# Partial sums of every second row tile of the fifth product kept in spare room of that product's w2 tiles

## The chip, the cores and the metric

The kernel runs on one core of a Trainium2 chip. The metric is the device time of one execution, in microseconds (us): the median of a few runs, and beside it one profiled execution whose trace shows every instruction. TensorE is called PE here, VectorE DVE, ScalarE ACT, GpSimd POOL, and SyncE, which mostly issues transfers, SP.

## What is computed

```python
xn = _layernorm(x)                                    # x: 1 x 2048 x 1024
s  = irfft2(rfft2(xn) * (w_r + 1j * w_i))             # a filter in the Fourier domain
g  = silu(silu(xn @ w1) @ w2)                         # w1: 1024 x 3584, w2: 3584 x 1024
return x + s * g
```

The change lies in the second matrix product of g, `h @ w2`, where h is `silu(xn @ w1)`.

## The kernel before

**The second product as seven.** `h @ w2` is not done in four blocks of 512 columns and half the rows, but by Strassen's scheme as seven smaller products, m = 0 to 6, of sums and differences of blocks. Each works on eight row tiles j = 0 to 7 of 128 rows and 512 columns. For each tile PE runs 42 matmuls into one PSUM tile `pb` (L539 to L541: 14 slices, three matmuls each, because operands are split into a high and a low f16 half): 21 with chunk k = 0 of the weights, 21 with chunk k = 1. Between the two chunks and after the second, other work may be put in.

**Weights.** `w2_gen` loads each slice of w2 into a tile `jr` (L412), and splits it: ACT writes the high half (L251, called from `split`), DVE the low half (L254). The halves go into `w2t[m, 0]` and `w2t[m, 1]`, seven slices each, in a ring of four buffers with the tag "big". The ring's buffers were made for `xnT` (2 x 8 x 512 f16, 16 KB in each partition), and a w2 tile of seven slices takes 14 KB of one. Two tiles to a product and four buffers to the ring: a tile of product 6 (the seventh) goes into the buffer that a tile of product 4 (the fifth) had. So the first write into `w2_6_0`, the split of slice 84 (`jr84`), must come after the last use of `w2_4_0`. The weights of product 6 are prepared while product 5 runs, and the first of those splits already during the last row tile of product 4.

**Partial sums.** In the fifth product, m = 4, each row tile adds its result to two earlier partial sums (`READS[4]` is (1, 0)). `load_parts` has SP load both from DRAM into tiles of 128x512 f32 (`pl`, L532): k = 1 (`pl4_j_1`, from `pd1_j`) and k = 0 (`pl4_j_0`, from `pd0_j`). DVE adds the PSUM tile to both (L596, L597). The k = 1 sum goes on through silu (L632), a product with the filter's result and an addition of x, and out (L626). The k = 0 sum goes back to `pd0_j` (L577, called from `keep`), to be used once more in product 6. Both tiles come from a ring of six, tag "pt". A row tile takes two of them, so a buffer comes back three row tiles later, and the load into it waits for the store out of it.

**The Fourier work beside it.** During products 0 to 6 a background queue feeds in the inverse transform. One pass over it (`i_gen`) has four first matmul groups `iu` (24 matmuls each, L1204 or L1212) into a ring of two PSUM tiles. Each group is evacuated by ACT (`uc`, L1218) and then by DVE (`ub`, L1220 and L1221). After some DVE arithmetic (`uu`), ACT writes the high half of `us` (L1283) and DVE the low half (L1284). Four second groups `id` (L1294) read all four `us` tiles. The third `iu` group can start only when DVE has emptied the first one's PSUM tile, and the fourth when the second one's is empty.

**Order and queues.** The order on each engine is fixed when the program is built: a rule feeds background work by estimated PE and DVE clocks. Stores are put off by a number of steps (`store`, `tick`): that of a k = 0 sum by three. Each engine runs its list in order, and a waiting instruction holds up what stands behind it. SP's transfers go on one queue, in the order of its list, and ACT issues the loads of h (`ht`, L515) in between its own work. Every transfer of SP or ACT reports to one of eight counters, DMAHW0 to DMAHW7; a wait in the lists below names the counter.

Of the kernel before, what the change touches and what calls it, by code (L numbers as in the profile page):

```python
# [9 lines left out]
F16 = mybir.dt.float16  # L10
F32 = mybir.dt.float32
# [116 lines left out]
def spectral_ffn(ctx, tc, x, w_r, w_i, w1, w2, ca, kc, ci, tw, pm, out):  # L128
    nc = tc.nc
# [12 lines left out]
    fp = ctx.enter_context(tc.tile_pool(name="fp", bufs=1))  # L142
    hstack = ExitStack()
    H = {"p": hstack.enter_context(tc.tile_pool(name="hid", bufs=1))}
    pf = ctx.enter_context(tc.tile_pool(name="pf", bufs=4, space=PSUM))
    pt = ctx.enter_context(tc.tile_pool(name="pt", bufs=2, space=PSUM))
# [5 lines left out]
    pd = {(k, j): dp.tile([128, 512], F32, name=f"pd{k}_{j}") for k in range(3) for j in range(8)}  # L152
# [38 lines left out]
    def store(tag, n, fn):  # L191

        d = [n, None]

        def run():
            held[tag].remove(d)
            fn()

        d[1] = run
        held.setdefault(tag, []).append(d)  # L200
        deferred.append(d)

    def tile_of(pool, shape, dtype, name, tag, bufs):
        while len(held.get(tag, ())) >= bufs - 1:
            d = held[tag][0]
            deferred.remove(d)
            d[1]()
        return pool.tile(shape, dtype, name=name, tag=tag, bufs=bufs)
# [35 lines left out]
    xnT, w1t, h32, w2t = {}, {}, {}, {}  # L244
# [5 lines left out]
    def high(hi, raw, scale):  # L250
        nc.scalar.activation(hi, raw, AF.Copy, scale=scale)  # L251

    def low(lo, raw, scale, hi):
        nc.vector.scalar_tensor_tensor(lo, raw, scale, hi, op0=OP.mult, op1=OP.subtract)  # L254
# [144 lines left out]
    def w2_block(m, q, b):  # L399
        r, h = W2_BLOCKS[m][b]  # L400
        return w2[(2 * q + r) * 128:(2 * q + r + 1) * 128, h * 512:(h + 1) * 512]

    def w2_gen():

        todo = [(m, q) for m in range(7) for q in range(NP)]
        raw = {}

        def load(n):
            if n < len(todo):
                m, q = todo[n]  # L410
                raw[n] = J["p"].tile([128, 512], F32, name=f"jr{n}", tag="jr", bufs=6)
                nc.sync.dma_start(raw[n], ws[m][q] if m in ws else w2_block(m, q, 0))  # L412

        def join(n):
            if n < len(todo) and todo[n][0] in SUMMED:
                nc.gpsimd.dma_start(raw[n], w2_block(*todo[n], 1), accum_op=OP.add)

        def split(n):
            m, q = todo[n]
            if q % 7 == 0:  # L420
                w2t[m, q // 7] = fp.tile([128, 7, 2, 512], F16, name=f"w2_{m}_{q // 7}", tag="big", bufs=4)
            high(w2t[m, q // 7][:, q % 7, 0], raw[n], sc2[:, q:q + 1])

        def rest(n):
            m, q = todo[n]
            w = w2t[m, q // 7][:, q % 7]
            low(w[:, 1], raw.pop(n), sc2[:, q:q + 1], w[:, 0])
            ready2[0] = n

        for n in range(4):  # L430
            load(n)
        yield 0
        yield 0
        for n, (m, q) in enumerate(todo):
            while q % 7 == 0 and (done2[0] < m - 1 or chunks[0] <= (3 if m else q // 7) and m < 2):
                if n and ready2[0] < n - 1:
                    rest(n - 1)
                yield 0
            load(n + 4)
            join(n + 2)  # L440
            split(n)
            if n and ready2[0] < n - 1:
                rest(n - 1)
            yield 0.1
        rest(n)
# [78 lines left out]
    def home(m, j):  # L524
        return ("kept", 8) if m == 6 and j >= 4 else ("pt", 6)

    def load_parts(m, j):
        for k in READS[m]:
            if (k, j) in part:
                continue  # L530
            t_ = tile_of(H["p"], [128, 512], F32, f"pl{m}_{j}_{k}", *home(m, j))
            nc.sync.dma_start(t_, pd[k, j])  # L532
            part[k, j] = t_

# [24 lines left out]
    def ahead_rows(m, j):  # L559
        g, p = j // 4, j % 4  # L560
        for c, h in FINALS[m]:
            tags = (("kept", 8), ("kept", 8)) if m == 6 else (("fs", 3), ("fx", 2))
            if m == 6 and j >= 4:
                tags = (("kept", 8), ("fs", 3) if h else ("fx", 2) if j < 7 else ("pt", 6))
            if (2 * g + c, p) in stile and (2 * g + c, p, h) not in rows:
                rows[2 * g + c, p, h] = rows_for(2 * g + c, p, h, H["p"], tags)

    def acc(m, j, ps, cols=slice(0, 512)):
        tt = nc.vector.tensor_tensor
        g, p = j // 4, j % 4  # L570
        ahead_rows(m, j)

        def fresh(name):
            return tile_of(H["p"], [128, 512], F32, f"{name}_{j}", "pt", 6)

        def keep(k, t_):
            store("pt", 3, lambda: nc.sync.dma_start(pd[k, j], t_))  # L577

        def evac():
            if m == 0:  # L580
                kept[j] = H["p"].tile([128, 512], F32, name=f"kept{j}", tag="kept", bufs=8)
                nc.scalar.activation(kept[j], ps, AF.Copy)
            elif m == 1:
                t_ = fresh("c11")
                tt(t_, kept[j], ps, op=OP.subtract)
                keep(0, t_)
            elif m == 2:
                tt(kept[j], kept[j], ps, op=OP.add)
            elif m == 3:
                t_ = fresh("c21")  # L590
                nc.scalar.activation(t_, ps, AF.Copy)
                tt(kept[j], kept[j], ps, op=OP.subtract)
                keep(1, t_)
            elif m == 4:
                t_, u = part.pop((1, j)), part.pop((0, j))
                tt(t_, t_, ps, op=OP.add)  # L596
                tt(u, u, ps, op=OP.add)  # L597
                keep(0, u)
                return final(2 * g + 1, p, 0, t_)
            elif m == 5:  # L600
                t_ = fresh("c12")
                nc.scalar.activation(t_, ps, AF.Copy)
                tt(kept[j], kept[j], ps, op=OP.add)
                keep(2, t_)
                return final(2 * g + 1, p, 1, kept.pop(j))
            else:
                t_, u = part[2, j][:, cols], part[0, j][:, cols]
                tt(t_, t_, ps, op=OP.subtract)  # L608
                tt(u, u, ps, op=OP.add)
                tag = home(m, j)[0]  # L610
                a_, b_ = final(2 * g, p, 1, t_, cols, tag), final(2 * g, p, 0, u, cols, tag)

                def both():
                    x_, y_ = a_(), b_()
                    return (lambda: (x_ and x_(), y_ and y_(), None)[2]) if x_ or y_ else None

                return both

        return evac
# [8 lines left out]
    def final(c, p, h, o, cols=slice(0, 512), tag=None):  # L628
        tag = tag or ("kept" if h and c % 2 else "pt")

        def act():
            nc.scalar.activation(o, o, AF.Silu, scale=c2)  # L632
            if (c, p) not in stile:
                store(tag, 1, lambda: nc.sync.dma_start(gd[c, p, h], o))
                fins[c, p, h] = True
                return None
            t_ = rows.get((c, p, h)) or rows_for(c, p, h, H["p"], (("fs", 3), ("fx", 2)))
            return lambda: finish_out(tag, c, p, h, o, *(v[:, cols] for v in t_), cols)

        return act  # L640
# [778 lines left out]
    with tc.manual_schedule():  # L1419
# [134 lines left out]
        for n, (m, j) in enumerate(seq):  # L1554
# [14 lines left out]
            for k in range(2):  # L1569
                while ready2[0] < m * NP + 7 * k + 6:  # L1570
                    slot(wq)
                mm2(m, j, ps, k)
                if k == 0:
                    settle()
                    load_parts(m, j)
                    ahead_rows(m, j)
                    if (m, j) == (6, 6):
                        load_parts(m, 7)
                        ahead_rows(m, 7)
                    tick()  # L1580
                    work()
# [43 lines left out]
```

## Time and profile before

| | |
|---|---|
| median of 3 runs | 1237.54 us (1236.69 to 1238.83) |
| the profiled execution | 1235.84 us, of which 1234.1 us span |
| DVE busy | 999.0 us, 81% of the span |
| ACT busy | 467.6 us, 38% |
| product 4 (the fifth) on PE | from about 984 to 1063 us of the span |
| moved by DMA | 293.67 MB, 238 GB/s on average |
| transfers `pd<-pl` in this stretch (8), issue to landing | 3.2 to 7.7 us, median 6.5 |

Times in the rows of a trace count from the start of the span. A row of a timeline gives the start, the length, the engine, the line and the operation, and in brackets the idle time of the engine before it with what ended that. A matmul's length is modelled, and matmuls overlap; for PE the distance from start to start counts.

### The profile page before, as it was taken

What the parts mean: (1) busy time and instruction counts of PE and PEld (TensorE: products, weight loads), DVE (VectorE), ACT (ScalarE), POOL (GpSimd) and SP (SyncE); (2) the same over time, 40 slices, a digit from 0 to 9 for tenths busy, and PEclk for the clock granted to TensorE, in tenths of its full rate; (3) what the DMA queues carried; (4) which work ended last, traced back from release to release, by engine and by line L of the source; (5) the groups of instructions that cost most, each with busy time, mean ns of one, the idle gap of its engine ahead of it and who ended that gap; (6) DMA issues with size and microseconds to landing.
All of it is one profiled execution on the core that took longest, in us unless ns stands there. A gap on an engine that the chain in (4) does not pass through costs nothing.

```text
span 1234.1 us, 19097 instructions
## 1 busy us (share of the span) xinstructions
PE 1220.7 (99%) x7033; PEld 625.2 (51%) x7033; DVE 999.0 (81%) x1970; ACT 467.6 (38%) x614; POOL 117.3 (10%) x245
## 2 busy tenths in 40 slices
PE   8999999999999999999999999999999999999998
PEld 5545445444544454445545555554455555555545
DVE  7687988899798898896969899985186678798886
ACT  4865344333554565444433222122032222243212
POOL 2330000001000000010001121114111111000000
PEclk9999999999999999999999999999999999999999
DMA  7487476655758898759898999997989999998576
GB/s 253 134 172 187 135 224 201 185 152 161 223 172 237 276 283 242 217 177 279 207 283 224 283 259 198 276 256 246 293 207 278 286 289 331 315 332 325 200 261 260
DMA packets 271102, 293.67 MB, mean 238 GB/s; under 512 B 40096, under 2 KB 198816, under 8 KB 270624
## 3 DMA queue, kind: packets, MB, share of 16 engines
q1 hardware_dynamic: 250992, 233.66, 65.7%
q10 hardware_dynamic: 15984, 51.45, 12.0%
q0 software_dynamic: 4032, 7.34, 3.5%
q8 instruction: 55, 0.90, 0.3%
q14 instruction: 39, 0.32, 0.1%
HBM read 185.95 MB, written 102.25 MB: 234 GB/s over the span
## 4 chain that ended last, share of the span: by engine, by line
PE 75%; DVE 11%; DMA 9%; issue 2%; ACT 1%; SPq 0%; POOL 0%; DVEq 0%; ACTq 0%; POOLq 0%
PE pa L456 45%; PE pb L539 8%; PE pb L541 8%; PE pb L540 8%; DVE Z L1055 2%; DMA wq<-in_A_w_i_dram 2%; DMA sd<-s 2%; PE id L1294 2%; DMA zd<-zq 1%; DMA ht<-hd_sum_d 1%; DVE T L1020 1%; DVE w L254 1%; PE iu L1204 1%; ACT xp L709 1%; PE iu L1212 1%
## 5 line engine op out<-in xcount | busy, mean ns | idle before, releaser
L456 PE MATMUL pa<-xnT,w 128*128 128x512 f16 x2688 | 585.2, 379 | 1.1 <-ACT w L251 0.7
L456 PEld LDWEIGHTS <-w 128*128 128x128 f16 x2688 | 262.2, 98 | 311.6 <-DVE w L254 1.3
L539 PE MATMUL pb<-w,ht 128*128 128x512 f16 (+2 forms) x812 | 300.4, 372 | 0.0
L540 PE MATMUL pb<-w,ht 128*128 128x512 f16 (+2 forms) x812 | 300.4, 372 | 0.0
L541 PE MATMUL pb<-w,ht 128*128 128x512 f16 (+2 forms) x812 | 300.3, 372 | 0.0
L541 PEld LDWEIGHTS <-ht 128*128 128x128 f16 x812 | 79.4, 98 | 91.0
L539 PEld LDWEIGHTS <-ht 128*128 128x128 f16 x812 | 79.5, 98 | 86.7
L540 PEld LDWEIGHTS <-ht 128*128 128x128 f16 x812 | 79.4, 98 | 86.7
L465 ACT ACTIVATE h<-pa,s 128x512 f32<-128x512 f32 x112 | 75.5, 678 | 122.9 <-PE pa L456 111.0
L251 ACT ACTIVATE w<-jr,sc 128x512 f16<-128x512 f32 x98 | 68.1, 713 | 77.8 <-PE pb L541 22.1
L254 DVE SCALAR_TENSOR_TENSOR w<-jr,sc,w 128x512 f16<-128x512 f32 x98 | 71.1, 744 | 2.1 <-ACT w L251 2.1
L254 DVE SCALAR_TENSOR_TENSOR hoone<-h,hs,hoone 128x2048 f16<-128x2048 f32 x28 | 65.6, 2344 | 7.9 <-ACT hoone L251 7.9
L251 ACT ACTIVATE hoone<-h,hs 128x2048 f16<-128x2048 f32 x28 | 56.0, 1998 | 36.5 <-DVE h L499 24.3
L251 ACT ACTIVATE hosum<-hr,hs 128x1536 f16<-128x1536 f32 x28 | 44.1, 1574 | 64.1 <-DVE hr L495 26.8
L981 ACT ACTIVATE zq<-Z,zs 128x1024 f16<-128x1024 f32 x16 | 18.4, 1149 | 103.9 <-DVE Z L1055 57.0
L494 DVE TENSOR_TENSOR hr<-h 128x1024 f32<-128x1024 f32 x28 | 34.2, 1221 | 24.4 <-ACT h L465 24.3
L254 DVE SCALAR_TENSOR_TENSOR hosum<-hr,hs,hosum 128x1536 f16<-128x1536 f32 x28 | 50.7, 1812 | 3.1 <-ACT hosum L251 3.1
L251 ACT ACTIVATE w<-w1r,rs 128x1024 f16<-128x1024 f32 x28 | 31.9, 1144 | 47.0 <-DVE w L254 31.8
L274 DVE TENSOR_REDUCE m<-w1r 128x1 f32<-128x1024 f32 x28 | 33.8, 1210 | 16.1 <-DMA w1r<-in_B_w_dram 16.1
L632 ACT ACTIVATE pl<-pl,c 128x512 f32<-128x512 f32 (+2 forms) x28 | 17.6, 657 | 70.1 <-DVE pl L608 41.6
L954 PE MATMUL fx<-vq,kq 128*128 128x256 f16 x192 | 43.2, 273 | 0.0
L955 PE MATMUL fx<-vq,kq 128*128 128x128 f16 x192 | 42.0, 219 | 0.0
(219 smaller groups left out, 1524.8 us busy)
## 6 DMA issues: line engine op xcount, KB each, us to landing
w1r<-in_B_w_dram SPq DMA_DIRECT2D x28, 512.0 KB, 6.2
hd_sum<-hosum SPq DMA_DIRECT2D x56, 256.0 KB, 2.9
hd_one<-hoone SPq DMA_DIRECT2D x56, 256.0 KB, 3.7
hd_dif<-hoone SPq DMA_DIRECT2D x56, 256.0 KB, 3.2
w2m<-in_B_w_dram SPq DMA_DIRECT2D x28, 512.0 KB, 5.2
ht<-hd_dif ACTq DMA_DIRECT2D x32, 448.0 KB, 6.3
jr<-in_B_w_dram SPq DMA_DIRECT2D x56, 256.0 KB, 6.8
ht<-hd_sum ACTq DMA_DIRECT2D x32, 448.0 KB, 6.4
```

Of the source, the lines that this page charges most:

```text
L251: nc.scalar.activation(hi, raw, AF.Copy, scale=scale)
L254: nc.vector.scalar_tensor_tensor(lo, raw, scale, hi, op0=OP.mult, op1=OP.subtract)
L274: nc.vector.tensor_reduce(m1[:, i:i + 1], raw[i], axis=AX.XY, op=OP.max, apply_absolute_value=True)
L456: nc.tensor.matmul(ps, w[:, wh, d], xt[:, xh, d], start=(n == 0), stop=(n == 23))
L465: nc.scalar.activation(hq[:, 2 * (c % 2) + f % 2], ps, AF.Silu, scale=s1[:, f:f + 1])
L494: tt(sums[:, 0:2], hq[:, 0::2], hq[:, 1::2], op=OP.subtract)
L539: nc.tensor.matmul(ps, hh[:, 0], w[:, 0], start=first, stop=False)
L540: nc.tensor.matmul(ps, hh[:, 0], w[:, 1], start=False, stop=False)
L541: nc.tensor.matmul(ps, hh[:, 1], w[:, 0], start=False, stop=last)
L954: nc.tensor.matmul(o, k[:, c, kh, 1], v[:, c, vh], start=(n == 0), stop=False)
L955: nc.tensor.matmul(ps[:, c, 0], k[:, c, kh, 2], v[:, c, vh, 128:256], start=False, stop=False)
L1055: eng.tensor_tensor(Z[:, ns, pos], x0[:, :, ls], x1[:, :, ls], op=o_)
```

## The change

The w2 tiles get room for an eighth slice, which no weight uses: 2 x 512 f16 in each partition, as many bytes as 512 f32. In product 4, for odd j, the k = 0 partial sum is loaded into that room instead of a tile of the "pt" ring: j = 1 and 5 into `w2_4_0`, j = 3 and 7 into `w2_4_1`. Its store back to DRAM is counted under the tag "big". The ring's buffers stay 16 KB.

```diff
         def split(n):
             m, q = todo[n]
             if q % 7 == 0:
-                w2t[m, q // 7] = fp.tile([128, 7, 2, 512], F16, name=f"w2_{m}_{q // 7}", tag="big", bufs=4)
+                w2t[m, q // 7] = fp.tile([128, 8, 2, 512], F16, name=f"w2_{m}_{q // 7}", tag="big", bufs=4)
...
         for k in READS[m]:
             if (k, j) in part:
                 continue
-            t_ = tile_of(H["p"], [128, 512], F32, f"pl{m}_{j}_{k}", *home(m, j))
+            if m == 4 and k == 0 and j % 2:
+                t_ = w2t[m, j // 2 % 2][:, 7].rearrange("p h x -> p (h x)").bitcast(F32)
+            else:
+                t_ = tile_of(H["p"], [128, 512], F32, f"pl{m}_{j}_{k}", *home(m, j))
             nc.sync.dma_start(t_, pd[k, j])
             part[k, j] = t_
...
         def keep(k, t_):
-            store("pt", 3, lambda: nc.sync.dma_start(pd[k, j], t_))
+            store("big" if m == 4 and j % 2 else "pt", 3, lambda: nc.sync.dma_start(pd[k, j], t_))
```

The instructions of all five engines stay the same, in the same order; line numbers behind L531 grow by three. What changes is which buffer some transfers use, and so what instructions wait for. Two places show it.

SP's list, from the second load for row tile 6 of product 4 (`pl4_6_0`) to the store of the k = 0 sum of row tile 5 (`pd0_5`). Before:

```order
L532 DMA pl4_6_0_10397<-pd0_6_104 128x512 [waits DMAHW6_49]
L556 DMA fs3_2_0_10399<-sd3_2_136 128x512 [waits DMAHW4_49]
L556 DMA fx3_2_0_10401<-in_A_x_dram 128x512 [waits DMAHW5_49,DVE_49]
L577 DMA pd0_4_102<-pl4_4_0_10137 128x512
L1354 DMA sd3_3_137<-s3_3_10354 128x1024 [waits DMAHW0_49]
L626 DMA out_0_dram<-pl4_4_1_10135 128x512 [waits DMAHW2_49]
L412 DMA jr87_10406<-in_B_w2_dram 128x512 [waits DMAHW3_49,DMASW1_49,Activation_49]
L532 DMA pl4_7_1_10463<-pd1_7_113 128x512 [waits DMAHW6_49,DMAHW4_49]
L532 DMA pl4_7_0_10465<-pd0_7_105 128x512 [waits DMAHW5_49,DMAHW2_49]
L556 DMA fs3_3_0_10467<-sd3_3_137 128x512 [waits DMAHW0_49]
L556 DMA fx3_3_0_10469<-in_A_x_dram 128x512 [waits DMAHW7_49,DVE_49]
L577 DMA pd0_5_103<-pl4_5_0_10304 128x512
```

With the change:

```order
L535 DMA pl4_6_0_10394<-pd0_6_104 128x512 [waits DMAHW3_49]
L559 DMA fs3_2_0_10396<-sd3_2_136 128x512 [waits DMAHW4_49]
L559 DMA fx3_2_0_10398<-in_A_x_dram 128x512 [waits DMAHW5_49,DVE_49]
L580 DMA pd0_4_102<-pl4_4_0_10135 128x512 [waits DMAHW6_49]
L1357 DMA sd3_3_137<-s3_3_10351 128x1024 [waits DMAHW0_49]
L629 DMA out_0_dram<-pl4_4_1_10133 128x512 [waits DMAHW2_49]
L412 DMA jr87_10403<-in_B_w2_dram 128x512 [waits DMAHW3_49,DMASW1_49,Activation_49]
L535 DMA pl4_7_1_10460<-pd1_7_113 128x512 [waits DMAHW4_49]
L535 DMA w2_4_1_9088<-pd0_7_105 128x512 [waits DMAHW5_49]
L559 DMA fs3_3_0_10463<-sd3_3_137 128x512 [waits DMAHW6_49,DMAHW0_49]
L559 DMA fx3_3_0_10465<-in_A_x_dram 128x512 [waits DMAHW7_49,DVE_49]
L580 DMA pd0_5_103<-w2_4_0_8680 128x512
```

Here `fs` and `fx` are rows of the filter's result and of x, `sd` the filter's rows in DRAM. Counted through the program: `pl4_6_0` waited for the store of `out` from row tile 3 (DMAHW6) and now waits for that of `pd0_3`. `pl4_7_1` waited for the store of `pd0_4`, and now waits only for the load `fs3_2`. `fs3_3` reads what the store `sd3_3` (DMAHW0) wrote, before and after. The store of `pd0_5` stands in the same place and waits for nothing of its own.

ACT's list, from the silu of row tile 6, past the evacuation of the second `iu` group, to a load of h (`ht`). Before:

```order
L632 ACTIVATE pl4_6_1_10395<-pl4_6_1_10395,c2_229 128x512 [waits DMAHW3_49]
L251 ACTIVATE w2_6_0_10564<-jr84_10220,sc2_230 128x512 [waits DMAHW6_49]
L1283 ACTIVATE us0_0_10591<-uu0_0_10528 128x1024 [waits DVE_49]
L1218 ACTIVATE uc0_1_10594<-iu0_1_10498 128x512 [waits PE_49,Activation_49]
L1264 ACTIVATE up0_1_10600<-ub0_1_10596 128x8 [waits DVE_49,Activation_49]
L1265 ACTIVATE up0_1_10600<-ub0_1_10596 128x8
L515 DMA ht5_2_0_10611<-hd_one_0_0_94 128x1792 [waits DMAHW4_49]
```

With the change:

```order
L635 ACTIVATE pl4_6_1_10392<-pl4_6_1_10392,c2_229 128x512 [waits DMAHW0_49]
L251 ACTIVATE w2_6_0_10560<-jr84_10218,sc2_230 128x512 [waits DMAHW6_49,DMAHW0_49]
L1286 ACTIVATE us0_0_10587<-uu0_0_10524 128x1024 [waits DVE_49]
L1221 ACTIVATE uc0_1_10590<-iu0_1_10494 128x512 [waits PE_49,Activation_49]
L1267 ACTIVATE up0_1_10596<-ub0_1_10592 128x8 [waits DVE_49,Activation_49]
L1268 ACTIVATE up0_1_10596<-ub0_1_10592 128x8
L515 DMA ht5_2_0_10607<-hd_one_0_0_94 128x1792 [waits DMAHW4_49]
```

The split of slice 84, the first write into `w2_6_0`, waited for its own load (DMAHW6). Now it also waits on DMAHW0 for the count that the store of `pd0_5` completes, since that store reads from the buffer `w2_6_0` is given. In the same way the first split into `w2_6_1`, that of slice 91, now waits for the store of `pd0_7`; `jr91` is loaded two transfers behind that store on SP's queue.

## The prediction

> **What bounds the kernel now.** I read the page's busy shares first, then PE's waits, the stretch of product 4, and the timelines of PE, DVE, ACT and SP around PE's one late wait.
>
> ```profile
> PE 1220.7 (99%) x7033; PEld 625.2 (51%) x7033; DVE 999.0 (81%) x1970; ACT 467.6 (38%) x614; POOL 117.3 (10%) x245
> PE tp L718 <- ACT x L709: 3.0, 3, 2.0
> PE iu L1212 <- DVE ub L1221: 1.7, 1, 1.7
> 984.00:1075.00 91.00, 89.28 (x565) 46.96 (x564) 70.34 (x161) 22.97 (x44) 7.51 (x9) 1.00 0.96 302
> ```
>
> PE is busy for 99% of the span, at full granted clock. Of its waits, the one on `iu` is the only one during the seven products; the others fall near the start, where the change does nothing. So the kernel is a chain of matmuls: an edit can win at most that wait, and loses whatever new gap it makes on PE. In the stretch of product 4 (window, then busy PE, PEld, DVE, ACT, POOL, clock, DMA share, GB/s) the DMA engines are 96% busy. Transfers are slow there.
>
> The old wait, followed back on the chain of waits (start, length, what):
>
> ```profile
> 1049.77 7.96 DMA out_dram<-pl
> 1057.75 3.87 DMA pl<-pd
> 1061.64 0.69 DVE pl L597
> 1062.33 0.60 DVE ub L1220
> 1062.93 0.61 DVE ub L1221
> ```
>
> ```profile
> 1061.48 0.38 PE L541 MATMUL pb<-w,ht 128*128 128x512 f16 x1
> 1063.59 1.55 PE L1212 MATMUL iu<-kk,zt 128*128 128x129 f16 x24 [1.72 <-DVE ub L1221]
> 1074.04 1.54 PE L1212 MATMUL iu<-kk,zt 128*128 128x129 f16 x24
> 1098.07 3.21 PE L1294 MATMUL id<-cis,us 128*128 128x130 f16 x48
> ```
>
> A store lands after 7.96 us and frees a "pt" buffer, the load of `pl4_6_0` starts, the second add of row tile 6 (L597) waits for it, and behind it on DVE stands the evacuation on which the third `iu` group waits. The rows at 1074.04 (fourth `iu` group) and 1098.07 (first two `id` groups) show no wait: they have slack, and the sum turns on how much.
>
> **Term 1, the wait removed.** Odd row tiles take one "pt" tile instead of two, so a buffer comes back later and its store is done.
>
> ```profile
> 1054.94 3.14 SPq L532 DMA_DIRECT2D pl<-pd  x2
> 1048.67 0.51 SPq L577 DMA_DIRECT2D pd<-pl  x1
> DMA to landing us min/median/max: 6.2/6.2/6.2
> DMA to landing us min/median/max: 4.8/4.8/4.8
> 1059.56 0.60 ACT L1218 ACTIVATE uc<-iu 128x512 f32<-128x512 f32 x1 [4.76 <-DMA pl<-pd]
> ```
>
> The first landing is that of the store issued at 1048.67 (`pd0_3`), so 1054.9; the second that of the load issued at 1054.94 (`pl4_6_1`). `pl4_6_0`, issued at 1057.75 before, now waits only for `pd0_3` and starts at 1054.9. At its neighbour's 4.8 us it lands at 1059.7 instead of 1061.6, 1.9 us earlier. L597 can then run at 1059.7, L1220 behind it 0.6 later at 1060.3 (ACT's copy, done at 1060.16, allows it), and PE's group follows at about 1061.6, where it is due at 1061.48 + 0.22. The gap of 1.7 us closes. If the busy queue gives the second load 0.9 us more, 0.8 is won. Bounds: 0.8 to 1.7; I take 1.7. The earlier loads of row tiles 3 to 5 cost or win nothing, since PE waits for none of their users.
>
> **Term 2, the wait added.** The split of slice 84 on ACT now waits for the store of `pd0_5`.
>
> ```profile
> 1063.79 0.71 ACT L632 ACTIVATE pl<-pl,c 128x512 f32<-128x512 f32 x1
> 1064.40 0.71 ACT L251 ACTIVATE w<-jr,sc 128x512 f16<-128x512 f32 x1
> 1066.53 1.06 ACT L1283 ACTIVATE us<-uu 128x1024 f16<-128x1024 f32 x1 [1.42 <-DVE uu L1277]
> 1067.49 0.58 ACT L1218 ACTIVATE uc<-iu 128x512 f32<-128x512 f32 x1
> 1068.75 0.42 SPq L556 DMA_DIRECT2D fs<-sd  x1
> 1069.69 0.43 SPq L577 DMA_DIRECT2D pd<-pl  x1
> DMA to landing us min/median/max: 6.9/6.9/6.9
> ```
>
> Before, the split ran at 1064.40. The store it must now follow was issued at 1069.69 and took 6.9 us: it landed at 1076.6, 12 us after the split. The data were ready long before (row tile 5's adds), but the store is put off three steps and stands on SP behind the loads of row tile 7.
>
> How early can the store be with the change? Ahead of it on SP stands `fs3_3`, which must wait for the store `sd3_3` to land.
>
> ```profile
> 1059.55 0.43 SPq L1354 DMA_DIRECT2D sd<-s  x1
> DMA to landing us min/median/max: 8.2/8.2/8.2
> 1058.13 0.42 SPq L556 DMA_DIRECT2D fs<-sd  x1
> 1049.22 0.51 SPq L1354 DMA_DIRECT2D sd<-s  x1
> DMA to landing us min/median/max: 7.9/7.9/7.9
> ```
>
> `fs3_2` was held until 1058.13 behind `pl4_6_0`; now its own wait, for `sd3_2`, is the last, 1049.22 + 7.9 = 1057.1, so SP is about 1.05 us earlier and `sd3_3` goes out at 1058.5. At 8.2 us it lands at 1066.7. `fs3_3` then starts, and by the distance in the rows above (1068.75 to 1069.69) the store of `pd0_5` 0.9 later, at 1067.6: 2.1 us earlier than before. Its landing, T0:
>
> ```profile
> DMA to landing us min/median/max: 3.2/6.5/7.7
> ```
>
> These are the eight such stores of product 4: T0 lies between 1070.8 and 1075.3. At its own 6.9 it would be 1074.5. But the transfers ahead of it are thinner now, and ACT, being stopped, doesn't issue its `ht` loads beside it; I take 5.7, between the smallest and the own value but nearer to the latter, so T0 = 1073.3. In a sentence by itself: the Trainium skill, "DMA: Bandwidth & Descriptors", section "Anatomy of one DMA — SWDGE (gpsimd) path", puts a DMA of GpSimd's queue at about 2.0 us plus its bytes over 436 GB/s, an estimate of 2.6 us for these 256 KB, by which T0 would be 1070.2 and the total below 3.1 us; the rows of this stretch, on SP's queue, show 6.9 us, and they decide.
>
> What is queued behind the split on ACT: the high half of `us0_0`, the evacuation `uc0_1`, then the `ht` loads for product 5. DVE waits for the first two, PE for DVE.
>
> ```profile
> 1067.62 1.23 DVE L1284 SCALAR_TENSOR_TENSOR us<-uu,us 128x1024 f16<-128x1024 f32 x1 [1.12 <-ACT us L1283]
> 1069.36 0.68 DVE L1221 TENSOR_TENSOR ub<-iu,uc 128x512 f32<-128x512 f32 x1
> 1062.85 0.68 DVE L1221 TENSOR_TENSOR ub<-iu,uc 128x512 f32<-128x512 f32 x1
> 1075.65 0.71 ACT L251 ACTIVATE w<-jr,sc 128x512 f16<-128x512 f32 x1
> 1076.27 1.04 ACT L1283 ACTIVATE us<-uu 128x1024 f16<-128x1024 f32 x1
> 1096.82 1.22 DVE L1284 SCALAR_TENSOR_TENSOR us<-uu,us 128x1024 f16<-128x1024 f32 x1 [1.02 <-ACT us L1283]
> ```
>
> First consequence, the fourth `iu` group. From a split to the next activation 0.62 (1075.65 to 1076.27), from `us` to L1221 of the next group 2.83 (1066.53 to 1069.36), from an L1221 to PE's start 0.74 (1062.85 to 1063.59): PE can start at T0 + 4.2 = 1077.5, against 1074.04 before. That is 3.5 us late (and a visible wait of 5.2, as PE arrives 1.7 early).
>
> Second consequence, the `id` groups. DVE's low half of `us0_0` moves from 1067.62 to T0 + 0.62 + 1.09 = 1075.0, so DVE is 7.4 us late. From there to the low half of `us0_3` at 1096.82 DVE is nearly always busy: its idle gaps are the about 1 us that ACT takes for each `us`, so I let the lag stay whole. `us0_3` is ready at 1098.04 + 7.4 = 1105.4. PE needs it after 18 of the 48 matmuls from 1098.07, that is 1.14 later (18/48 of about 3.05), at 1099.2. The slack is 1.15, and PE ends 7.4 - 1.15 = 6.2 us late: the first wait and a second of 2.7 us together, with term 1 already spent inside them. Bounds from T0 (late = T0 - 1067.1): 3.7 to 8.2.
>
> What is late next (the ending of product 5 on ACT, the landing of `ht` loads in this stretch, the splits on DVE):
>
> ```profile
> L602 ACT ACTIVATE c<-pb x8: 575/597/597, 1080.8 to 1153.0; 128x512 f32<-128x512 f32 x8
> DMA to landing us min/median/max: 3.8/6.6/11.2
> L254 DVE SCALAR_TENSOR_TENSOR w<-jr,sc,w x16: 741/746/752, 1052.0 to 1137.8; 128x512 f16<-128x512 f32 x16
> ```
>
> The late `ht5_2` loads cost nothing: issued at about T0 + 4.3 and landing some 6.6 later, at 1084.2, they are needed when product 5's third row tile starts. From the third `iu` group to the fourth, one group and one row tile of 42 matmuls, it is 10.45; from the fourth the same again leads to 1084.5, and 3.5 late to 1088.0. The wait of slice 91's split costs nothing either: its own load stands behind the same store. The splits of `w2_6` are over by 1138.5, and product 6 starts where ACT empties the last tile of product 5, at 1153: 15 us, which cover the lag.
>
> **Sum.** 1235.84 + 6.2 = 1242.0 for an execution like the profiled one. The median of the runs shown is 1.7 above that execution, so I predict 1243.7.
>
> **The rivals.**
> - *Only the first wait counts* (0.17): DVE makes up its lag before `us0_3`. For it: DVE is 81% busy over the span. Against it: hardly a gap between 1067 and 1097. Time: 1235.84 + 3.5 + 1.7 = 1241.0.
> - *The store is later or the delay spreads* (0.10): `sd3_3` takes the 9 us that such stores reach, `pd0_5` its 7.7, `ht5_2` comes late too. Late = 8.2 + 1, so about 1246.9.
> - *The added wait is covered* (0.13): this is the other side. The store lands before ACT's stop reaches PE; only term 1 is left: 1237.54 - 1.7 = 1235.8, and less if that too comes back as a wait. It decides only if T0 is below 1067.1, which is before the store can be issued by the rows above; it needs SP to be freed some 4 us earlier, by stores that land in 5 us instead of 8. Against it stands the 96% DMA share.
>
> That the change does nothing is no rival: the lists show the wait.
>
> **How the numbers follow.** The forecast, both waits, gets 0.60, with 1241.2 to 1245.7 from the bounds of T0 (1237.54 + 3.7 and + 8.2). Towards the first rival at a small T0 (1070.8 + 4.2 - 1074.04, about 1 late) the range reaches down to 1239.5, towards the second up to 1247. About 0.2%, 2.5 us, is what a measurement of this kernel tells from no change: 1235.06 to 1240.02. Slower: the forecast, the second rival and most of the first, 0.85. Same: most of the covered case, and the first rival at small T0, 0.11. Faster: 0.04, the covered case where other runs had more than 2.5 us to win.
>
> **What would show it.** Right: ACT's split L251 after the silu of row tile 6 idles some 9 to 11 us, ended by a DMA `pd<-w`; PE's waits have the `iu` line with some 5 us and the `id` line with 2 to 3, the latter ended by DVE `us`; the old 1.7 is gone; SP issues the store of `pd0_5` at about 1067 to 1068. Wrong: no such idle time on ACT, or PE waits below 2 us in all. If the `id` wait is missing, the DVE lag was made up.

## The result, and the profile after

The changed kernel takes 1241.85 us (median of 7 runs, 1238.52 to 1242.64), the kernel before, beside it, 1236.78 (7 runs, 1235.10 to 1238.83). The ratio is 1.0035, with a 95% interval of 1.0022 to 1.0048: slower, by about a third of a percent. The forecast was 1243.7, within 1239.5 to 1247. The profiled execution of the changed kernel took 1241.61, the one before 1235.84: 5.8 us more.

The span and busy times of the changed kernel's page, and the two waits of PE that the change brought (engine, line, what for, us in total, times, longest):

```profile
span 1239.8 us, 19084 instructions
PE 1223.0 (99%) x7033; PEld 626.3 (51%) x7033; DVE 998.7 (81%) x1970; ACT 467.6 (38%) x614; POOL 117.3 (9%) x245
PE iu L1215 <- DVE ub L1224: 3.4, 1, 3.4
PE id L1297 <- DVE us L1287: 0.8, 1, 0.8
```

The work is the same: PE has the same 7033 matmuls. The 1.7 us wait of before has gone from the list, and two others have come. ACT's timeline of the changed kernel shows what stopped, and SP's the store for which it waited, with the line that tells how long that store took:

```profile
1062.41 0.71 ACT L635 ACTIVATE pl<-pl,c 128x512 f32<-128x512 f32 x1
1072.09 0.72 ACT L251 ACTIVATE w<-jr,sc 128x512 f16<-128x512 f32 x1 [8.97 <-DMA pd<-w]
1072.72 1.04 ACT L1286 ACTIVATE us<-uu 128x1024 f16<-128x1024 f32 x1
```

```profile
1066.38 0.32 SPq L559 DMA_DIRECT2D fs<-sd  x1
1067.29 0.58 SPq L580 DMA_DIRECT2D pd<-w  x1
```

```profile
DMA to landing us min/median/max: 4.8/4.8/4.8
```

The split of slice 84 ran at 1064.40 before; now ACT stands for 8.97 us in front of it, ended by the store `pd<-w`, which is that of `pd0_5` out of `w2_4_0`'s room. With it wait the high half of `us0_0` (L1286) and everything behind. PE's timelines, first two rows of the kernel before that were not shown yet (the first pair of `iu` groups and the last `id` group), then the changed kernel's:

```profile
1054.42 2.91 PE L1212 MATMUL iu<-kk,zt 128*128 128x129 f16 x48
1111.71 1.69 PE L1294 MATMUL id<-cis,us 128*128 128x130 f16 x24
```

```profile
1054.89 2.91 PE L1215 MATMUL iu<-kk,zt 128*128 128x129 f16 x48
1062.21 1.55 PE L1215 MATMUL iu<-kk,zt 128*128 128x129 f16 x24
1072.44 0.38 PE L544 MATMUL pb<-w,ht 128*128 128x512 f16 x1
1076.27 2.21 PE L1215 MATMUL iu<-kk,zt 128*128 128x129 f16 x24 [3.45 <-DVE ub L1224]
1101.97 1.46 PE L1297 MATMUL id<-cis,us 128*128 128x130 f16 x20
1104.28 1.93 PE L1297 MATMUL id<-cis,us 128*128 128x130 f16 x28 [0.85 <-DVE us L1287]
1116.64 1.69 PE L1297 MATMUL id<-cis,us 128*128 128x130 f16 x24
```

The useful measure is the distance from the first pair of `iu` groups to the last `id` group: it holds all that the change touches on PE, and leaves out what varies elsewhere. It was 1111.71 - 1054.42 = 57.29 and is 1116.64 - 1054.89 = 61.75: 4.46 us more. The changed kernel was already 0.47 later at the first pair, where the change has done nothing for PE yet. The third group comes without its wait, 7.32 after the pair where it was 9.17. The wait at 1104.28 stands behind 20 of the 48 matmuls, the first that need the low half of `us0_3`. The rest of the 5.7 us by which the span grew is in the tail. The last DVE instructions of the two kernels, before first:

```profile
1231.17 0.29 DVE L624 TENSOR_TENSOR pl<-pl,fx 128x128 f32<-128x128 f32 x1
```

```profile
1236.10 0.29 DVE L627 TENSOR_TENSOR pl<-pl,fx 128x128 f32<-128x128 f32 x1
```

From the end of that row to the end of the span it was 1234.1 - 1231.46 = 2.64, and is 1239.8 - 1236.39 = 3.41: 0.77 more. So 0.47 + 4.46 + 0.77 = 5.7. Between the last `id` group and that last add both kernels take the same 119.75; the 0.77 comes from the last store of `out`, which SP issues right behind the add and which lands after 1.5 us before and 2.4 us with the change.

One more row, the stretch behind the 3.45 us gap in the changed kernel (window, busy PE, PEld, DVE, ACT, POOL, granted clock, DMA share, GB/s):

```profile
1076.00:1080.00 4.00, 3.73 (x29) 2.64 (x30) 3.84 (x11) 1.05 (x3) 0.00 (x0) 0.62 0.65 203
```

The granted clock fell to 0.62 there, and the fourth `iu` group took 2.21 us where it took 1.54. The prediction had nothing of this.

### The profile page after: what moved, and what is told of

It is laid out like the page before. It is cut to its first block, busy times and chain, and to the rows that moved or that the text cites. A ratio compares the mean times of both kernels' runs of the same rounds, so it can differ in the third digit from the quotient of the medians.

```text
span 1239.8 us, 19084 instructions
## 1 busy us (share of the span) xinstructions
PE 1223.0 (99%) x7033; PEld 626.3 (51%) x7033; DVE 998.7 (81%) x1970; ACT 467.6 (38%) x614; POOL 117.3 (9%) x245
```

## The experiments

All start from the changed kernel unless it is said otherwise. The runs of the kernel before that were made beside them had medians of 1236.49 us (29 runs; e1 to e4), 1237.44 (29 runs; a_again, e5 to e7) and 1237.41 (25 runs; e8 to e10). Single runs of it spread over 8 us and more, so the distances inside the profiles decide as much as the medians.

### e1: the sums of row tiles 5 and 7 in other rooms

```diff
-                t_ = w2t[m, j // 2 % 2][:, 7].rearrange("p h x -> p (h x)").bitcast(F32)
+                t_ = w2t[4 + j // 4, j // 2 % 2][:, 7].rearrange("p h x -> p (h x)").bitcast(F32)
```

> The partial sums of row tiles 5 and 7 go to the rooms of the next product's w2 (w2_5_0, w2_5_1), those of 1 and 3 stay in w2_4_0 and w2_4_1; all else as in the changed kernel. If the loss comes from ACT's split of slice 84 waiting for the store of pd0_5: that split now waits only for the store of pd0_1, landed long before, so ACT stands still under 1 us there, the fourth iu group starts without a wait, the id group too, and the gap of 1.7 us of the kernel before stays closed as well: 1.2 to 1.9 us under the kernel before, near 1235. If instead sums of odd row tiles in w2's rooms cost by themselves (their traffic next to the weights, or the earlier loads and stores): slower than before as the changed kernel, near 1241.5.

Measured: 1237.90 us (12 runs), ratio 1.0008 (0.9995 to 1.0020). Its PE and ACT rows:

```profile
1058.81 2.91 PE L1215 MATMUL iu<-kk,zt 128*128 128x129 f16 x48
1066.79 0.71 ACT L251 ACTIVATE w<-jr,sc 128x512 f16<-128x512 f32 x1
1114.21 1.69 PE L1297 MATMUL id<-cis,us 128*128 128x130 f16 x24
```

The split has no wait, no `iu` or `id` group of this pass waits, and pair to last group is 55.40: 6.35 less than the changed kernel, 1.89 less than the kernel before. That fits the added wait, and the 1.7 of the old one. Yet the median shows no gain over the kernel before. In this profile PE came to the pair 4.4 us later than in the kernel before. The loss lies at 843 us, far ahead of the change, where the program runs 18 small matmuls (`eps`) that wait for POOL: the first of them starts 1.0 us later than in the kernel before (844.21 for 843.20), and the next `iu` group, at 899.9 for 895.5, is 4.4 later. The timeline's row, then the window's:

```profile
844.21 0.40 PE L1088 MATMUL eps<-edge,perm 128*128 128x24 f32 x2 [0.92 <-POOL edge L1081]
```

```profile
848.00:852.00 4.00, 4.00 (x10) 1.36 (x9) 3.13 (x5) 1.58 (x3) 3.58 (x11) 0.50 0.73 169
```

Behind a wait of 0.92 us and these small matmuls the granted clock was 0.50. The kernel before's profile had 1.00 there. This was not one odd run: the mean granted clock was 0.998 or less in 10 of e1's 12 runs, and in 8 of the 29 runs of the kernel before beside them (the median of those 8 was 1239.9 us, of the other 21 it was 1235.6). Whether the rooms make the drop more frequent is not shown. e7 to e10 take this up.

### e2: the store two steps earlier

```diff
-            store("big" if m == 4 and j % 2 else "pt", 3, lambda: nc.sync.dma_start(pd[k, j], t_))
+            store("big" if m == 4 and j % 2 else "pt", 1 if m == 4 and j == 5 else 3, lambda: nc.sync.dma_start(pd[k, j], t_))
```

> The changed kernel, with the store of row tile 5's sum put off by one step and not three. By the added wait: the store is issued 5 to 8 us earlier, lands before ACT reaches slice 84 (about 1062 to 1064), ACT's wait of 8.97 us on that split is under 1 us, and the time is 1.2 to 1.9 us under the kernel before, near 1235. If the place in w2_4_0 is what costs, whatever the store's time: no change to the changed kernel, near 1241.5. If the sum is not ready one step after its product, SP stands still in the middle and something else is late: over 1242.

Measured: 1238.01 us (12 runs, 1235.90 to 1241.32), ratio 1.0011 (0.9998 to 1.0025). It lies between the two numbers that the theories gave. The profiled execution was the slowest of the 12. The timeline's rows of SP, PE and ACT, the line on the store's landing, and two rows of the DMA issues between 1055 and 1073 us (KB each, median us to landing):

```profile
1062.73 0.32 SPq L580 DMA_DIRECT2D pd<-w  x1
1056.27 2.91 PE L1215 MATMUL iu<-kk,zt 128*128 128x129 f16 x48
1071.61 0.72 ACT L251 ACTIVATE w<-jr,sc 128x512 f16<-128x512 f32 x1 [6.06 <-DMA pd<-w]
1116.17 1.69 PE L1297 MATMUL id<-cis,us 128*128 128x130 f16 x24
```

```profile
DMA to landing us min/median/max: 8.9/8.9/8.9
```

```profile
ht<-hd_one ACTq DMA_DIRECT2D x2, 448.0 KB, 7.0
sd<-s SPq DMA_DIRECT2D x1, 512.0 KB, 9.7
```

The store went out 6.46 us after the pair, where it was 12.40 in the changed kernel: 5.9 earlier. It landed only 1.9 earlier (split at 15.34 after the pair, where it was 17.20), because it took 8.9 us and not 4.8. These two `ht` loads and the `sd` store, 1.4 MB, had been issued within 3.2 us ahead of it (from 1059.61 on), and between them a load of `fx` and two more stores of 256 KB each. That all this is what held it up is an inference from the times, not tried. The expectation that an early store lands early was wrong. In the place itself 1.85 us were won (59.90 for 61.75). The median is 3.8 under the changed kernel's, in different sets of runs; whether the store lands earlier in the faster runs no trace shows.

### e3 and e4: row tile 5 alone, and all but row tile 5

```diff
-            if m == 4 and k == 0 and j % 2:
+            if m == 4 and k == 0 and j == 5:
```

> Of the four sums only that of row tile 5 lies in w2's room. By the added wait: the old wait of 1.7 us at the third iu group comes back, since row tile 6's load waits for the store of a result again, and the store of pd0_5 is issued at about 1069.7 as in the kernel before, landing at 1074.5 to 1076.6; ACT's split waits 11 to 13 us, the fourth iu group's wait is 5 to 8 us, and the whole is 7 to 9 us over the kernel before: 1244 to 1246. If the store's issue does not move the time (the loss is a fixed price of the clock's drop after a wait): about 5 us over, 1242. If four sums together make the loss by their traffic: a quarter of it, 1238.

```diff
-            if m == 4 and k == 0 and j % 2:
+            if m == 4 and k == 0 and j in (1, 3, 7):
```

> The sums of row tiles 1, 3 and 7 lie in w2's rooms, that of 5 in its old ring. By the added wait: slice 84 waits for nothing new, the old wait of 1.7 us comes back (the ring turns so that row tile 6's load meets the store of a result), and slice 91's wait for the store of pd0_7 costs nothing: within 1 us of the kernel before, 1236 to 1237.5. If each sum in a room costs alike: three quarters of the loss, near 1240.5. If slice 91's wait stops ACT where someone waits for it: over 1240, with a PE wait ended by DVE at about 1105 or later.

(The condition of the store's tag is changed in the same way in each.) Measured: e3 1244.49 us (6 runs), ratio 1.0059 (1.0041 to 1.0076); e4 1236.77 (12 runs), ratio 1.0004 (0.9991 to 1.0017). The whole loss comes with the sum of row tile 5; the three others together cost nothing that can be told. Neither their number nor their traffic counts, and slice 91's wait for `pd0_7` is free, as predicted. e3's time is the one that was expected, but in part by luck: ACT's stop was to be 11 to 13 us and the fourth `iu` group's wait 5 to 8, and they are 8.73 and 2.28; what they lack came from elsewhere, 1.64 us from a slow clock (the table below). Rows of e3, then of e4:

```profile
1058.51 2.91 PE L1215 MATMUL iu<-kk,zt 128*128 128x129 f16 x48
1074.49 0.72 ACT L251 ACTIVATE w<-jr,sc 128x512 f16<-128x512 f32 x1 [8.73 <-DMA pd<-w]
1106.68 2.81 PE L1297 MATMUL id<-cis,us 128*128 128x130 f16 x28 [0.97 <-DVE us L1287]
1120.68 1.69 PE L1297 MATMUL id<-cis,us 128*128 128x130 f16 x24
```

```profile
1053.92 2.91 PE L1215 MATMUL iu<-kk,zt 128*128 128x129 f16 x48
1061.20 1.54 PE L1215 MATMUL iu<-kk,zt 128*128 128x129 f16 x24
1047.62 0.51 SPq L629 DMA_DIRECT2D out_dram<-pl  x1
1109.32 1.69 PE L1297 MATMUL id<-cis,us 128*128 128x130 f16 x24
```

One part of both expectations failed: the old wait did not come back. e4's third group stands 7.28 after the pair, with no wait, though its load for row tile 6 does wait for the store of `out` from row tile 3, as in the kernel before. That store went out at 1047.62, 6.30 ahead of the pair, where it was 1049.77, 4.65 ahead, in the kernel before: with two tiles fewer in the ring, row tile 5's loads no longer wait for the store of `out` from row tile 2, and SP gets there sooner (counted through the program). So the old wait closes in more than one way. In e3 that load waits only for the store of `pd0_3`; the expectation had misread the ring.

### a_again and e5: the slow clock filled

The changed kernel once more, beside a version with 28 matmuls that nobody reads, ahead of the fourth `iu` group (the rest of the added lines keeps the program's estimate of PE's clock as it was, so that the order stays the same):

> The changed kernel once more, beside the runs that follow. As before: 4 to 6 us over the kernel before, about 1241.5. From the start of the first two iu groups to the last id group in the profile: 61 to 63 us, against 57.29 in the kernel before and 55.40 with the sums of row tiles 5 and 7 in other rooms.

```diff
         def mat(g):
+            if c == 0 and g == 3:
+                sp_ = pf.tile([128, 512], F32, name="spin2", tag="ff")
...
+                for _ in range(28):
+                    nc.tensor.matmul(sp_[:, 0:256], idle[:, 0:128], idle, start=True, stop=True)
...
             ps = pt.tile([128, 1024], F32, name=f"iu{c}_{g}", tag="ft")
```

> The changed kernel with 28 matmuls of 256 columns added on TensorE, whose results nobody reads, just ahead of the fourth iu group, where TensorE stands still for 3.4 us; all other engines have the same instructions in the same order. They fill about 3.0 us of the gap, so the granted clock should stay near 1.00 where it was 0.62, and the fourth group should take 1.55 us and not 2.21. If the second wait (of the id group, for DVE) sets the end and the slow clock was hidden ahead of it: that wait grows from 0.8 to about 2.5 us and the time stays at the changed kernel's, within 1 us. If the slow clock is part of the loss: 1.5 to 2 us faster than the changed kernel.

Measured: a_again 1244.00 us (6 runs), ratio 1.0051 (1.0031 to 1.0070); e5 1241.89 (12 runs), ratio 1.0035 (1.0019 to 1.0051). The intervals overlap, so the timing alone does not tell them apart. Rows of a_again, then of e5, and e5's window behind the gap:

```profile
1054.20 2.91 PE L1215 MATMUL iu<-kk,zt 128*128 128x129 f16 x48
1069.87 0.72 ACT L251 ACTIVATE w<-jr,sc 128x512 f16<-128x512 f32 x1 [8.75 <-DMA pd<-w]
1074.05 2.42 PE L1215 MATMUL iu<-kk,zt 128*128 128x129 f16 x24 [1.96 <-DVE ub L1224]
1114.42 1.69 PE L1297 MATMUL id<-cis,us 128*128 128x130 f16 x24
```

```profile
1057.62 2.91 PE L1221 MATMUL iu<-kk,zt 128*128 128x129 f16 x48
1072.94 0.72 ACT L251 ACTIVATE w<-jr,sc 128x512 f16<-128x512 f32 x1 [8.18 <-DMA pd<-w]
1075.34 3.22 PE L1202 MATMUL spin<-ones 128*128 128x256 f16 x28
1078.39 1.54 PE L1221 MATMUL iu<-kk,zt 128*128 128x129 f16 x24
1117.49 1.69 PE L1303 MATMUL id<-cis,us 128*128 128x130 f16 x24
```

```profile
1076.00:1080.00 4.00, 4.00 (x50) 3.63 (x48) 3.88 (x11) 1.05 (x3) 0.00 (x0) 1.00 0.45 117
```

The added matmuls held the clock at 1.00, and the fourth group took 1.54. But from ACT's split to the last `id` group it is 44.55 in both (1114.42 - 1069.87, and 1117.49 - 1072.94), as it is in the changed kernel (1116.64 - 1072.09). Here, then, a slow clock in front of a wait that ends later anyway costs nothing. The second wait in e5 was expected at 2.5 and is 1.0: the added matmuls ran 1.3 us past the time at which the fourth group could have started (4.2 after the split, at 1077.1), and so took that much of its place.

The table sets the profiles side by side (us; "split" is the start of ACT's split of slice 84, "pair" the first two `iu` groups, "last" the last `id` group):

| kernel | split - pair | last - pair | last - split |
|---|---|---|---|
| changed | 17.20 | 61.75 | 44.55 |
| a_again | 15.67 | 60.22 | 44.55 |
| e5, clock held | 15.32 | 59.87 | 44.55 |
| e2 | 15.34 | 59.90 | 44.56 |
| e3 | 15.98 | 62.17 | 46.19 |
| before, no wait at the split | 9.98 | 57.29 | |
| e1 and e4, no wait at the split | 7.98 and 6.34 | 55.40 and 55.40 | |

Four profiles, of three kernels, with one constant to within 0.01, over landings 1.9 us apart: every microsecond by which the store lands later makes PE a microsecond later. e3 has 1.64 on top: there the clock fell behind the last wait, where nothing covers it. It shows first in the 28 matmuls of the `id` group (2.81 us for 1.93 in the changed kernel); from their start to the next `id` group it is 7.94 for 6.30.

### e6: only the splits moved

The store and the room stay; the first splits of `w2_6` are held back by two slices.

```diff
-            while q % 7 == 0 and (done2[0] < m - 1 or chunks[0] <= (3 if m else q // 7) and m < 2):
+            while q % 7 == 0 and (done2[0] < m - 1 or m == 6 and q == 0 and not late[0] or chunks[0] <= (3 if m else q // 7) and m < 2):
...
+            late[0] = (m, j) >= (5, 0)
             after(acc(m, j, ps))
```

> The changed kernel with the store and the room left as they are; only the splits of product 6's w2 are held back by two slices, so that slice 84's stands on ACT behind the work that the store of pd0_5 delayed. If it is ACT's stop at that split and nothing about the room or the store that costs: ACT does not stand still there, no PE wait at the fourth iu group, and 4 to 6 us less than the changed kernel, near 1235 to 1237. If the store itself or its place costs: no change, near 1241.5. If w2 of product 6 becomes ready too late: a wait ended by ACT or DVE w at the start of product 6.

Measured: 1236.59 us (12 runs), ratio 0.9985 (0.9971 to 1.0000).

```profile
1058.19 2.91 PE L1215 MATMUL iu<-kk,zt 128*128 128x129 f16 x48
1077.51 0.72 ACT L251 ACTIVATE w<-jr,sc 128x512 f16<-128x512 f32 x1 [0.50 <-DMA pd<-w]
1113.60 1.69 PE L1297 MATMUL id<-cis,us 128*128 128x130 f16 x24
```

The store lands later than in any other profile with that sum in `w2_4_0`, 19.3 after the pair, and the split still waits 0.50 for it. But `us0_0` and `uc0_1` no longer stand behind it, and pair to last group is 55.41, as if there were no such wait. So the landing matters only through what stands behind the split on ACT. No wait at the start of product 6 appeared.

### e7 to e10: the clock at 843 us

To e1 (e7, and once more e10), to the kernel before (e8) and to the changed kernel (e9) eight matmuls that nobody reads are added among the 18 small ones:

```diff
...
         for n in range(3):
+            for _ in range(4 if n < 2 else 0):
+                nc.tensor.matmul(ps[:, 512:768], idle[:, 0:128], idle, start=True, stop=True)
...
```

> As e1_rooms_apart, with eight matmuls of 256 columns added on TensorE, whose results nobody reads, among the 18 small eps matmuls at 843 us: there e1_rooms_apart's profile had a wait of 0.9 us and then a granted clock of 0.50 to 0.69 for 8 us, which the kernel before's profile had not. If that slow clock is what spreads the runs over 1234 to 1240 us and hides the gain of 1.1 to 1.9 us: the clock stays at 1.00 there, the runs come closer together, and the median is 0.5 to 2 us under e1_rooms_apart and 1 to 2 us under the kernel before. If the spread has another cause: about e1_rooms_apart's 1237.9, plus up to 0.9 for the added matmuls.

> The kernel before, with the eight unread matmuls of 256 columns among the eps matmuls, as in e7_keep_warm; no room is used. If all of e7_keep_warm's 2.0 us come from the clock held at 843 us: as fast as it, near 1235.0. If the rooms without the late store bring their 1.1 to 1.9 us besides (1.7 us of PE wait at the third iu group): 1.1 to 1.9 us slower than the kernel with rooms and warm matmuls, near 1236.5, and that wait is in the profile.

> The changed kernel with the same eight matmuls. If the drop of the clock at 843 us is only noise beside the change: 4 to 6 us slower than e8_before_warm, with a narrower spread than the changed kernel alone. If the change makes that drop more frequent and its loss is partly that: within 3 us of e8_before_warm. In the profile the last id group starts 44.55 us after ACT's split of slice 84, as in the four profiles so far whose PE waits end before it.

> e7_keep_warm once more beside these two: the sums of row tiles 5 and 7 in the rooms of the next product's w2, and the eight matmuls. 1.5 to 2.5 us under the kernel before; from the first iu groups to the last id group 55.40 us, against 57.29 in e8_before_warm if that has its wait of 1.7 us.

| kernel | median us | range us, runs | ratio to before, 95% |
|---|---|---|---|
| e7, rooms apart, warm | 1235.43 | 1234.76 to 1238.74, 12 | 0.9979 (0.9967 to 0.9991) |
| e10, the same | 1235.59 | 1234.63 to 1239.97, 12 | 0.9993 (0.9981 to 1.0006) |
| e8, before, warm | 1237.79 | 1235.04 to 1241.27, 12 | 0.9999 (0.9986 to 1.0011) |
| e9, changed, warm | 1241.95 | 1241.06 to 1243.63, 7 | 1.0037 (1.0024 to 1.0051) |

The stretch of e7 that answers to the slow one of e1, and the third `iu` group of e8:

```profile
848.00:852.00 4.00, 4.00 (x20) 1.79 (x19) 1.99 (x4) 0.42 (x1) 3.78 (x15) 1.00 0.99 356
```

```profile
1062.79 1.55 PE L1216 MATMUL iu<-kk,zt 128*128 128x129 f16 x24 [0.89 <-DVE ub L1225]
```

In e7 the clock stayed at 1.00, and 2 of 12 runs had a mean granted clock of 0.998 or less, where e1 had 10. With the rooms apart the matmuls brought the median down by 2.5 us (1237.90 to 1235.43, in different sets of runs). Alone they did nothing for the kernel before: e8 has its spread still, so that has another cause, which stays open. e8's old wait was 0.89 in this profile, not 1.72: the gap that the change closes varies. e9 lies 4.2 us over e8, so the change's loss is no effect of the drop at 843. The constant of 44.55 did not hold in e9: from the split at 1070.78 to the last group at 1116.99 it is 46.21, again with the clock falling behind the waits of the `id` group, as in e3.

The kernel of e7 and e10 is the best of the study: both medians are 1.8 to 2.0 us under the kernel before. One interval lies below 1, the other includes it.

## Why the prediction was right, and where its sizes were off

- **Term 1, the old wait closes: right.** The third `iu` group comes without a wait in the changed kernel, in a_again, e1, e3, e4 and e5. e2 had 0.93 there; why was not followed. The mechanism was told too narrowly (one store that falls away from one load); e4 shows that SP's earlier start of the whole chain does it too.
- **Term 2, ACT stops at the split of slice 84: right.** Idle time of 8.97 us ended by `pd<-w`, where 9 to 11 was written. That this stop is the cause is shown from four sides: another room for the sum (e1), that one sum alone (e3), all but it (e4), and the split moved behind the work it blocked (e6).
- **T0, mis-sized by 1.7.** The store was put at 1067.6 and went out at 1067.29, which is 1066.8 in the kernel before's time (0.47 less). It took 4.8 us where 5.7 was taken. So T0 was 1071.6, not 1073.3; the bounds of 1070.8 to 1075.3 held it. One reason given for a shorter store, thinner transfers ahead of it, is not to be seen in the DMA share: while the store was under way the DMA share was 1.00, and 0.89 in the kernel before, where it took 6.9 us. The store's time is not a property of the store: the same 256 KB took 4.0 (e5), 4.2 (e9), 4.3 (a_again), 4.7 (e3), 6.3 (e6) and 8.9 us (e2). What sets it was not tried.
- **Late = T0 - 1067.1: right to 0.1.** 1071.6 - 1067.1 = 4.5, and 4.46 were measured. DVE's lag did stay whole: its low half of `us0_0` and that of `us0_3` were both 5.7 us late (1073.79 for 1067.62 and 1103.00 for 1096.82, less 0.47). The slack was 5.7 - 4.46 = 1.25 and not 1.15: PE needs the low half of `us0_3` after 20 matmuls, as the row of the `id` group shows, and not after 18. The table shows the constant in four profiles.
- **The two waits, 5.2 and 2.7 forecast, 3.4 and 0.8 seen.** The first is short by the 1.7 us of T0 (from landing to the fourth group it is 4.2, as written). The second would have been 2.7 even so; from the fourth `iu` group to the first `id` group the changed kernel took 25.70 us and the kernel before 24.03, so the slow clock had taken 1.67 of the wait's place. This step the prediction lacked; it changes how the loss shows, not its size.
- **The Trainium skill's price for a DMA of GpSimd's queue,** about 2.0 us plus bytes over 436 GB/s ("DMA: Bandwidth & Descriptors", section "Anatomy of one DMA — SWDGE (gpsimd) path"), gives an estimate of 2.6 us for these 256 KB. No run here puts this store on that queue; on SP's queue the runs show 4.0 to 8.9 us.
- **The sum, 1.85 too high in the median.** Over the profiled execution 6.2 was forecast and 5.8 measured: 1.7 less from T0, and 0.47 + 0.77 more from places that the prediction did not name. The rest is the 1.7 added because the median stood that much over the profiled execution; the changed kernel's stands 0.24 over its own. That the forecast for the profiled execution came within 0.4 us is therefore in part luck: 1.7 too much and 1.24 too little.
- **The two small terms.** The 0.47 at the first pair is small beside what other profiles vary there (1053.9 to 1056.3 where the clock stayed at 1.00 at 843 us). The 0.77 in the tail hardly looks like chance: from the last `id` group to the end it is 123.2 to 123.3 us in the changed kernel, a_again, e1, e2, e5, e7, e9 and e10, 123.0 in e4, and 122.3 to 122.4 in the kernel before, e3, e6 and e8. It goes with the landing of the last store of `out`; what makes that store take longer stays open.
- **The rivals.** That only the first wait counts is out (the table's constant holds at the last group), the covered wait is out (8.97 us of idle time), and so is a store later than forecast (T0 lay 1.7 below it, and PE waited for no `ht` load); the time of this last one adds up to 1237.54 + 9.2 = 1246.7, not 1246.9.

## What to carry to other kernels

Spare bytes in a ring's buffer are not free: what is put there ties its last use to the buffer's next writer. Look up who writes that buffer next, on which in-order engine, and what stands behind that writer; the room is free only if its last reader (here a store put off by three steps) is done before. Where a transfer must land sooner, look at what is queued ahead of it too: in e2 issuing it 5.9 us earlier brought 1.9.

## What was not expected of the hardware

The granted clock of PE falls after shorter gaps than the 3.45 us of the changed kernel's. It fell after that one (0.62 over the next 4 us), after one of 1.96 us in a_again (the `iu` group took 2.42 us for 1.54), after two of 1.36 and 0.97 us close together in e3's `id` group, and after 0.92 us followed by 18 small matmuls in e1 (0.50). In e6 these 18 matmuls had a wait of 0.2 us only, and the clock fell there as well:

```profile
848.00:852.00 4.00, 4.00 (x13) 1.53 (x12) 3.87 (x5) 2.05 (x4) 3.21 (x8) 0.60 0.76 235
```

It did not fall after 1.72 us in the kernel before, nor after 2.28 and 2.40 us ahead of the fourth `iu` group of e3 and e9, nor in e2 after 1.37 and 0.97 us in the `id` group. So the length of the wait alone does not decide it. The rows behind the gap of the changed kernel:

```profile
1078.27 0.63 PE L542 MATMUL pb<-w,ht 128*128 128x512 f16 x1
1078.70 0.63 PE L543 MATMUL pb<-w,ht 128*128 128x512 f16 x1
```

The Trainium skill ("TensorE: Matmul & The Clock Gate", section "Part 1: The HAM clock gate (the "warmup" mystery)") names a free-running window of about 3.4 us and half rate after an idle one. Half rate fits: these matmuls of 512 columns start 0.43 us apart, and 0.22 apart ahead of the gap. A free-running window would make the drop depend on where the gap falls, which fits the mixed cases; but a wait of 1.96 us is no whole idle window, so here less than that was enough.

What such a drop costs depends on what follows: nothing where a later wait takes it up (changed kernel, a_again); where none does, 1.6 us in e3 and e9, and in e1 3.4 us between the first small matmul and the next `iu` group.
